# Block-sparse attention with a gated feed-forward: batches 1 to 3 go from masked full scores to gathered key blocks

## The chip, the cores and the metric

The kernel runs on one core of a Trainium2 chip. The core has a matrix engine (PE), three elementwise engines (DVE, ACT and POOL) and a queue engine (SP); SP, ACT and POOL also issue DMA transfers. Each engine works through its own instructions in program order and waits on semaphores for the others. The metric is the device time of one execution in microseconds (us); lower is better. A measurement of this kernel can tell a difference of about 0.2% from none.

## The reference

There are 4 batches, 8 heads, 768 positions and a head size of 64. Positions form 24 blocks of 32. A query block sees its own block and its two neighbours, the first and the last block, and three sampled blocks; the queries of the first and last block see everything. The attention output, as 3072 rows of 512, goes through an RMS norm and a gated feed-forward of width 1536.

```python
    scores = scale * np.matmul(q, k.transpose(0, 1, 3, 2))
    mask = np.abs(blk_i - blk_j) <= window            # window = 1
    mask = mask | (blk_i == 0) | (blk_j == 0) | (blk_i == n_blocks - 1) | (blk_j == n_blocks - 1)
    for qb in range(n_blocks):
        for kb in sampled_blocks[qb]:
            mask[qb * block:(qb + 1) * block, kb * block:(kb + 1) * block] = True
    scores = np.where(mask, scores, -1000000000.0)
    attn = np.exp(scores - np.max(scores, axis=-1, keepdims=True))
    attn = attn / (np.sum(attn, axis=-1, keepdims=True) + 1e-09)
    out = np.matmul(attn, v)
    ...
    rms = np.sqrt(np.mean(x * x, axis=-1, keepdims=True) + 1e-06)
    xn = x / rms * rms_g
    g = xn @ w_gate
    silu = g * (1.0 / (1.0 + np.exp(-g)))
    return silu * (xn @ w_val) @ w_out
```

## The kernel before, in words

All scores are computed, and the mask is part of the matmul: below the 64 rows of a head, `KT` and `QT` hold 24 more rows, which say of each key its block and give each query -65536 for every block that it does not see. A matmul over 88 rows so yields masked scores, and the exponential makes the masked ones zero.

Tokens are handled in groups: batch 0 in three groups of 2 tiles of 128 tokens, batches 1 to 3 in two groups of 3 tiles each (`groups`). For a group and a head, `scores` multiplies six blocks of 128 keys (L330, 256 or 384 columns) and takes the exponential on ACT (L333, 768 columns a piece). One head later `pv` multiplies the exponentials with `Vp`, whose column 64 is one, so that column 64 of `op` is the sum (L341, 66 columns); DVE divides (L350, L351). Sums of squares (L375, DVE), the power -1/2 (L383, POOL) and a scaling (L395, L403) give `xs`, which is transposed into `xg` by DMA from SP, or on PE for the first groups and the last.

The feed-forward of a group is cut into pieces by `ffn_pieces`: `gate` (four matmuls, L442, then tanh on ACT, L446), `val` (four matmuls, L453, then two DVE operations into `hps`, L457 and L459) and `down` (three matmuls into `yp`, L470, and at last ACT's copy and the store). Gate, value and down results share three PSUM buffers (`ps_f`). The order is written out by hand: the pieces of the group that was finished last are spread over the "positions" between the scores and values of the present one (`enter`, `position`), so that PE always has work while ACT takes exponentials.

q and k of batch 0 are transposed on PE. Those of batches 1 to 3 are loaded by POOL, transposed by DMA from SP (`turn`, L300) and moved into `KT` and `QT` by two more DMAs each (`place`, L308). v is loaded by POOL and cast by DVE (`cast_v`, L120). `KT`, `QT` and `Vp` have two buffers each, by the parity of the batch.

Of the kernel before, what the change touches and what calls it, by code (L numbers as in the profile page):

```python
# [18 lines left out]
def kernel(  # L19
# [11 lines left out]
):  # L31

    nc = tc.nc
    P = 128
    B, H, S, D = q.shape
    NB = S // 32  # L40
    NC = S // P
    DM = H * D
    DFF = moe_w_gate.shape[1]
    KD = DM // P
    MASKV = -65536.0
    SCALE = 1.0 / (D ** 0.5)
    NRND = sampled_blocks.shape[1]
    NF = DFF // P
    HC = NC // 2
    TGM = HC * P  # L50

    groups = [(0, c, 2) for c in range(0, NC, 2)]
    groups += [(b, c, HC) for b in range(1, B) for c in range(0, NC, HC)]
    FIRST = NC // 2
    KR = D + NB
    NP = H // 2
    VW = D + 2
    VS = D + 16
# [6 lines left out]
    work = ctx.enter_context(tc.tile_pool(name="work", bufs=1))  # L65
    ps_f = ctx.enter_context(tc.tile_pool(name="ps_f", bufs=3, space=bass.MemoryType.PSUM))
# [3 lines left out]


    qbf, kbf, vraw, qrest = {}, {}, {}, {}

    def load_q0(pr, lo, hi):

        if lo == 0:
            t = qbf[(0, pr)] = ld.tile([P, 2, 2 * D], BF16, name="q0", tag="q0", bufs=3)
        else:
            t = ld.tile([P, 2, NC * D], BF16, name="qbf", tag="qbf", bufs=4)[:, :, lo * D:]
            qrest[(0, pr)] = t  # L80
        nc.gpsimd.dma_start(  # L81
            out=t, in_=q[0, 2 * pr:2 * pr + 2].rearrange(
                "e (p c) d -> p e (c d)", p=P)[:, :, lo * D:hi * D])

    def load_one(b, pr, store, t=None):
        src, name = (k, "kbf") if store is kbf else (q, "qbf")
        if t is None:
            t = ld.tile([P, 2, NC * D], BF16, name=name, tag=name, bufs=4)
        nc.gpsimd.dma_start(  # L89
            out=t,  # L90
            in_=src[b, 2 * pr:2 * pr + 2].rearrange("e (p c) d -> p e (c d)", p=P))
        store[(b, pr)] = t

    def load_qk(b, pr):
        load_one(b, pr, kbf)
        load_one(b, pr, qbf)

    def load_v(b, pr):
        t = ld.tile([P, 2, NC, D], FP32, name="vraw", tag="vraw" if b else "vraw0",
                    bufs=2 if b else 4)  # L100
        nc.gpsimd.dma_start(  # L101
            out=t, in_=v[b, 2 * pr:2 * pr + 2].rearrange("e (p c) d -> p e c d", p=P))
        vraw[(b, pr)] = t
# [3 lines left out]
    wo = persist.tile([P, NF, DM], BF16, name="wo")  # L107
    def load_gv(lo, hi):

# [5 lines left out]
    KT = [persist.tile([P, H, S], BF16, name=f"KT{i}") for i in range(2)]  # L115
    QT = [persist.tile([P, H, S], BF16, name=f"QT{i}") for i in range(2)]
    Vp = [persist.tile([P, H, NC, VS], BF16, name=f"Vp{i}") for i in range(2)]

    def cast_v(b, pr, eng):
        eng.tensor_copy(  # L120
            out=Vp[b % 2][:, 2 * pr:2 * pr + 2, :, 0:D], in_=vraw.pop((b, pr)))
# [3 lines left out]
    samp_i = const.tile([32, NB * NRND * 2], I32, name="samp_i")  # L125
# [3 lines left out]
    nc.scalar.dma_start(out=samp_i[0:NB, :], in_=s32.to_broadcast([NB, NB * NRND * 2]))  # L129
    first = {}  # L130
    for h in range(2):
        for which, src in ((0, k), (1, q)):
            f32 = ld.tile([P, NC * D], FP32, name="first", tag="turned", bufs=4)
            cols = 2 * D if which else NC * D
            nc.sync.dma_start(
                out=f32[:, 0:cols],
                in_=src[0, h].rearrange("(p c) d -> p (c d)", p=P)[:, 0:cols])
# [5 lines left out]
    def halves(which, b):  # L143

        if which == 0:
            return KT[b % 2][0:D].rearrange("p h (w c s) -> p h w c s", w=2, s=P)
        return QT[b % 2][0:D].rearrange("p h (c w s) -> p h w c s", w=2, s=P)

    def first_turn(src, which):
        dt = src.dtype  # L150
        t = ps_f.tile([P, HC, P], dt, name="tfirst", tag="ff")
        for cc in range(1 if which else HC):
            nc.tensor.transpose(
                out=t[:, cc, :], in_=src[:, 2 * cc * D:(2 * cc + 2) * D],
                identity=ident32 if dt == FP32 else ident)
        return t

    def first_copy(h, which, t, w, copy):
        hi = 1 if which else HC
        copy(out=halves(which, 0)[:, h, w, 0:hi, :], in_=t[w * D:(w + 1) * D, 0:hi])  # L160

    idle = const.tile([P, 512], BF16, name="idle")
# [3 lines left out]

# [15 lines left out]
    ki_i = work.tile([32, S], I32, name="ki_i", tag="hps", bufs=2)  # L182
# [16 lines left out]
    for i in range(2):  # L199
        nc.vector.memset(Vp[i][:, :, :, D:VW], 1.0)  # L200
# [12 lines left out]
    kind = KT[0][D:KR, 0, :]  # L213
    qmask = QT[0][D:KR, 0, :]
# [3 lines left out]

# [9 lines left out]
    for lo, hi in ((2, 4), (4, H)):  # L228
        nc.sync.dma_start(out=KT[0][D:KR, lo:hi, :],
# [20 lines left out]
    def spread_queries(third, lo):  # L250
# [3 lines left out]
            out=QT[0][D:KR, lo:H, c_lo:c_hi],  # L254
# [5 lines left out]
    def copy_rows(T, m, lo, hi, c_lo, c_hi):  # L260

        nc.vector.tensor_copy(
            out=T[0][D:KR, lo:hi, c_lo:c_hi],
# [10 lines left out]
    copy_rows(QT, qmask, 1, 2, 0, 2 * P)  # L274
    copy_rows(KT, kind, 1, 2, 0, S)
    nc.sync.dma_start(out=rmsr, in_=moe_rms_g.rearrange("(h p) -> h p", p=P))

    def transpose_qk(b, pr, which, lo, hi, spare, copy):

        src = (qrest if lo else qbf if which else kbf)[(b, pr)]
# [7 lines left out]
        view = halves(which, b)[:, 2 * pr:2 * pr + 2]  # L290
# [3 lines left out]
    turned = {}  # L294

    def turn(b, pr, which):

        src = (kbf if which == 0 else qbf).pop((b, pr))
        t = ld.tile([P, 2, HC, P], BF16, name="turned", tag="turned", bufs=4)
        nc.sync.dma_start_transpose(  # L300
            out=t.rearrange("p e c s -> p (e c) s"), in_=src.rearrange("p e x -> p (e x)"))
        turned[(b, pr, which)] = t

    def place(b, pr, which):
        t = turned.pop((b, pr, which))
        view = halves(which, b)[:, 2 * pr:2 * pr + 2]
        for w in range(2):
            nc.sync.dma_start(out=view[:, :, w], in_=t[w * D:(w + 1) * D])  # L308

    def place_half(b, pr, which, w):  # L310
        t = turned[(b, pr, which)]
        view = halves(which, b)[:, 2 * pr:2 * pr + 2]
        nc.vector.tensor_copy(out=view[:, :, w], in_=t[w * D:(w + 1) * D])
        if w:
            del turned[(b, pr, which)]

    def ex_tile(n):
        t = work.tile([P, NC * TGM], BF16, name="ex", tag="ex", bufs=3)
        return t[:, 0:NC * n * P].rearrange("p (j t) -> p j t", j=NC)

    def scores(grp, h, part, ex):

        b, c0, n = grp
        tg = n * P
        nj = 2 if n == HC else 3
        st = ps_s.tile([P, 1024], FP32, name="st", tag="st")
        at = st.rearrange("p (j t) -> p j t", t=512 if n == HC else tg)
        for e in range(nj):
            jt = nj * part + e
            nc.tensor.matmul(  # L330
                out=at[:, e, 0:tg], lhsT=KT[b % 2][0:KR, h, jt * P:(jt + 1) * P],
                rhs=QT[b % 2][0:KR, h, c0 * P:c0 * P + tg], start=True, stop=True)
        nc.scalar.activation(  # L333
            out=ex[:, nj * part:nj * (part + 1), :], in_=at[:, 0:nj, 0:tg], func=AF.Exp,
            scale=SCALE)

    def values(grp, h, ex, op):
        b, c0, n = grp
        for it in range(n):
            for jt in range(NC):  # L340
                nc.tensor.matmul(  # L341
                    out=op[:, it, 0:VW], lhsT=ex[:, jt, it * P:(it + 1) * P],
                    rhs=Vp[b % 2][:, h, 2 * (jt % HC) + jt // HC, 0:VW], start=(jt == 0), stop=(jt == NC - 1))

    def pv(grp, h, ex, stage):
        n = grp[2]
# [149 lines left out]
    fill = []  # L496
# [334 lines left out]
```

## Time and profile before

| | |
|---|---|
| median of 3 runs | 309.09 us (308.88 to 309.12) |
| the profiled execution | 309.93 us |
| its span, first to last instruction | 308.2 us |
| mean granted PE clock | 0.998 |
| matmuls | 2843 |
| DMA moved | 36.71 MB, mean 119 GB/s |

The profile is of one execution, and its span is a little shorter than the time, which also holds what lies around the first and last instruction. A line of a group of instructions gives the line of the code, engine, operation, output and inputs with shapes and count, then the busy time in us and the mean length of one in ns, then the idle time of the engine ahead of them and what ended it. A matmul's own length contains the way through the array; how far apart matmuls start is read from the chain or the timeline. A line of a stage gives busy times of all engines in a stretch.

### The profile page before, as it was taken

What the parts mean: (1) busy time and instruction counts of PE and PEld (TensorE: products, weight loads), DVE (VectorE), ACT (ScalarE), POOL (GpSimd) and SP (SyncE); (2) the same over time, 40 slices, a digit from 0 to 9 for tenths busy, and PEclk for the clock granted to TensorE, in tenths of its full rate; (3) what the DMA queues carried; (4) which work ended last, traced back from release to release, by engine and by line L of the source; (5) the groups of instructions that cost most, each with busy time, mean ns of one, the idle gap of its engine ahead of it and who ended that gap; (6) DMA issues with size and microseconds to landing.
All of it is one profiled execution on the core that took longest, in us unless ns stands there. A gap on an engine that the chain in (4) does not pass through costs nothing.

```text
span 308.2 us, 7249 instructions
## 1 busy us (share of the span) xinstructions
PE 299.9 (97%) x2843; PEld 198.9 (65%) x2863; DVE 203.6 (66%) x561; ACT 204.8 (66%) x330; POOL 54.7 (18%) x81
## 2 busy tenths in 40 slices
PE   8889999999999999999999999999999999999995
PEld 6676886985787566656666566655666566655653
DVE  7788884885578567763768457682767546675860
ACT  4886775776888677757776676676767667732331
POOL 9846201042220212012200122010000100010000
PEclk9999999999999999999999999999999999999999
DMA  7999999999999478526673379614000130002002
GB/s 124 276 210 201 208 215 151 171 173 245 218 205 146 112 154 162 109 48 189 113 156 85 81 176 148 140 25 139 16 2 0 42 115 2 0 5 100 2 0 103
DMA packets 61082, 36.71 MB, mean 119 GB/s; under 512 B 38348, under 2 KB 56640, under 8 KB 61048
## 3 DMA queue, kind: packets, MB, share of 16 engines
q0 software_dynamic: 17120, 17.90, 32.7%
q1 hardware_dynamic: 43892, 18.35, 27.5%
q8 instruction: 22, 0.36, 0.5%
q14 instruction: 12, 0.10, 0.1%
q10 hardware_dynamic: 36, 0.01, 0.0%
HBM read 28.59 MB, written 6.29 MB: 113 GB/s over the span
## 4 chain that ended last, share of the span: by engine, by line
PE 91%; POOL 3%; DMA 3%; DVE 2%; issue 1%; ACT 0%; POOLq 0%
PE gp L442 21%; PE vp L453 20%; PE yp L470 20%; PE st L330 18%; PE op L341 11%; DMA qbf<-in_q_dram 3%; POOL kbf L89 1%; PE tx L424 1%; POOL vraw L101 1%; POOL q L81 1%; DVE junk L375 1%; DVE stage L368 0%; PE tqk L287 0%; DVE xs L403 0%; POOL ki_i L183 0%
## 5 line engine op out<-in xcount | busy, mean ns | idle before, releaser
L333 ACT ACTIVATE ex<-st 128x768 bf16<-128x768 f32 x186 | 150.0, 813 | 53.7 <-PE st L330 51.9
L330 PE MATMUL st<-QT,KT 88*128 88x384 bf16 (+1 forms) x432 | 93.9, 309 | 1.4 <-DVE QT L292 1.0
L442 PE MATMUL gp<-xg,wg 128*128 128x384 bf16 (+1 forms) x432 | 80.8, 307 | 0.0
L453 PE MATMUL vp<-xg,wv 128*128 128x384 bf16 (+1 forms) x432 | 80.2, 307 | 0.0
L457 DVE SCALAR_TENSOR_TENSOR u<-th,gp 128x384 bf16<-128x384 bf16 (+1 forms) x108 | 54.8, 508 | 38.1 <-ACT th L446 36.6
L470 PE MATMUL yp<-wo,hps 128*128 128x512 bf16 (+1 forms) x283 | 71.9, 369 | 0.9
L446 ACT ACTIVATE th<-gp 128x384 bf16<-128x384 f32 (+1 forms) x108 | 49.1, 454 | 27.8 <-PE gp L442 27.5
L459 DVE TENSOR_TENSOR hps<-u,vp 128x384 bf16<-128x384 bf16 (+1 forms) x108 | 55.1, 510 | 11.3
L330 PEld LDWEIGHTS <-KT 88*128 88x128 bf16 x432 | 41.5, 98 | 26.1 <-DVE QT L292 2.0
L453 PEld LDWEIGHTS <-wv 128*128 128x128 bf16 x432 | 40.6, 97 | 20.6 <-issue 0.2
L442 PEld LDWEIGHTS <-wg 128*128 128x128 bf16 x432 | 40.1, 97 | 20.5 <-issue 0.3
L341 PEld LDWEIGHTS <-ex 128*128 128x128 bf16 x1116 | 42.8, 97 | 8.4 <-issue 0.2
L341 PE MATMUL op<-Vp,ex 128*128 128x66 bf16 x1116 | 44.9, 193 | 0.0
L470 PEld LDWEIGHTS <-hps 128*128 128x128 bf16 x300 | 27.6, 97 | 22.6 <-DMA wo<-in_moe_w_out_dram 0.3
L383 POOL TENSOR_TENSOR rstd<-ssq,mhalf 128x3 f32<-128x3 f32 (+1 forms) x9 | 7.4, 817 | 143.1 <-DVE ssq L375 143.1
L350 DVE RECIPROCAL rz<-op 128x3 f32<-128x3 f32 (+1 forms) x64 | 11.2, 174 | 24.0 <-PE op L341 23.7
L476 ACT ACTIVATE yo<-yp 128x512 f32<-128x512 f32 (+1 forms) x25 | 14.4, 577 | 15.4 <-PE yp L470 15.4
L351 DVE TENSOR_TENSOR stage<-op,rz 128x192 bf16<-128x192 f32 (+1 forms) x64 | 21.8, 341 | 2.2
L101 POOL DMA_DIRECT2D vraw<-in_v_dram x16 | 11.8, 739 | 59.3 <-DVE Vp L120 55.7
L375 DVE CUSTOM_DVE_ANT_0 junk<-stage 128x448 bf16<-128x448 bf16 (+1 forms) x24 | 14.7, 611 | 0.5
L395 DVE SCALAR_TENSOR_TENSOR xs<-stage,rstd,gain 128x512 bf16<-128x512 bf16 x15 | 10.4, 746 | 4.4 <-POOL rstd L383 4.4
L89 POOL DMA_DIRECT2D qbf<-in_q_dram x12 | 8.6, 721 | 16.8 <-DMA turned<-qbf 15.4
(71 smaller groups left out, 112.2 us busy)
## 6 DMA issues: line engine op xcount, KB each, us to landing
vraw<-in_v_dram POOLq DMA_DIRECT2D x16, 384.0 KB, 5.2
out_dram<-yo SPq DMA_DIRECT2D x23, 256.0 KB, 2.3
kbf<-in_k_dram POOLq DMA_DIRECT2D x15, 192.0 KB, 6.0
qbf<-in_q_dram POOLq DMA_DIRECT2D x12, 192.0 KB, 6.3
KT<-turned SPq DMA_DIRECT2D x24, 96.0 KB, 3.7
QT<-turned SPq DMA_DIRECT2D x22, 96.0 KB, 2.9
wg<-in_moe_w_gate_dram POOLq DMA_DIRECT2D x4, 384.0 KB, 10.7
wv<-in_moe_w_val_dram POOLq DMA_DIRECT2D x4, 384.0 KB, 12.1
```

Source lines behind the costliest of these rows:

```text
L101: nc.gpsimd.dma_start(out=t, in_=v[b, 2 * pr:2 * pr + 2].rearrange("e (p c) d -> p e c d", p=P))
L330: nc.tensor.matmul(out=at[:, e, 0:tg], lhsT=KT[b % 2][0:KR, h, jt * P:(jt + 1) * P], rhs=QT[b % 2][0:KR, h, c0 * P:c0 * P + tg], start=Tru ...
L333: nc.scalar.activation(out=ex[:, nj * part:nj * (part + 1), :], in_=at[:, 0:nj, 0:tg], func=AF.Exp, scale=SCALE)
L341: nc.tensor.matmul(out=op[:, it, 0:VW], lhsT=ex[:, jt, it * P:(it + 1) * P], rhs=Vp[b % 2][:, h, 2 * (jt % HC) + jt // HC, 0:VW], start=(j ...
L351: nc.vector.tensor_tensor(out=stage[:, 0:n, h * D:(h + 1) * D], in0=op[:, 0:n, 0:D], in1=rz[:, 0:n].unsqueeze(2).to_broadcast([P, n, D]), ...
L375: nc.vector.tensor_tensor_reduce(out=junk[:, 0:hi - lo], in0=part, in1=part, scale=1.0, scalar=(e["ssq"][:, it:it + 1] if lo else DM * 1e- ...
L442: nc.tensor.matmul(out=gp[:, 0:tg], lhsT=wg[:, c, f * P:(f + 1) * P], rhs=xg[:, c, 0:tg], start=(c == 0), stop=(c == KD - 1))
L446: nc.scalar.activation(out=th[:, 0:tg], in_=gp[:, 0:tg], func=AF.Tanh, scale=0.5)
L453: nc.tensor.matmul(out=vp[:, 0:tg], lhsT=wv[:, c, f * P:(f + 1) * P], rhs=xg[:, c, 0:tg], start=(c == 0), stop=(c == KD - 1))
L457: nc.vector.scalar_tensor_tensor(out=u[:, 0:tg], in0=th[:, 0:tg], scalar=1.0, in1=gp[:, 0:tg], op0=ALU.add, op1=ALU.mult)
L459: nc.vector.tensor_tensor(out=hps[:, f, 0:tg], in0=u[:, 0:tg], in1=vp[:, 0:tg], op=ALU.mult)
L470: nc.tensor.matmul(out=yp, lhsT=hps[:, f, tt * P:(tt + 1) * P], rhs=wo[:, f, lo:hi], start=(f == 0), stop=(f == NF - 1))
```

## The change

Batch 0 stays as it was. Batches 1 to 3 are cut into chunks of four query blocks: five regular chunks of four neighbouring blocks (2 to 5, 6 to 9, ...) and one edge chunk with blocks 0, 23, 1 and 22, which makes 18 chunks (`chunks`).

Keys are laid out in pairs: `KT` now has an even position's 64 values in partitions 0 to 63 and the next one's in 64 to 127, so a block of 32 keys is 16 columns. For each query block, 8 blocks of keys are copied side by side into 128 columns of `kg`: three sampled, the first, three of the window, the last. The window and the first and last block are copied by DVE (`gather_k`); the sampled blocks by ACT or POOL with an address from a register (`sampled_k`), which `addresses` loads earlier. `gather_q` (DVE) lays the queries out twice in `Qd`, once for each half of the partitions, with zeros in the other, so one matmul of 128 x 128 by 64 columns scores a query block against its 256 keys (`scores`, four bursts a chunk with an exponential of 512 columns each). An edge chunk scores its two full rows against all keys.

Values are cast into `Vs`, stored to a table in DRAM (`table`), and POOL gathers 128 rows of 2112 bytes for each query block by indirect DMA with the indices `vidx` (`gather_v`). A sampled block that is seen already, or sampled twice, points to rows of zeros, sums included. `values` multiplies with 32 columns of weights at a time: `op[j * 32:(j + 1) * 32]` for the four blocks in turn, 66 columns each.

A chunk is scored in one iteration, its values are taken in the next, which has ten positions, and feed-forward groups are of 2, 3, 3, 3, 3, 2 and 2 chunks. q and k of batches 1 to 3 are transposed on PE and copied by DVE (batch 1) or ACT. Loads of v for batches 2 and 3 move from POOL to SP. `KT0`, `QT0` and `Vp` of batch 0 share memory with buffers of the sparse part.

```diff
-    KT = [persist.tile([P, H, S], BF16, name=f"KT{i}") for i in range(2)]
-    QT = [persist.tile([P, H, S], BF16, name=f"QT{i}") for i in range(2)]
-    Vp = [persist.tile([P, H, NC, VS], BF16, name=f"Vp{i}") for i in range(2)]
+    KT = [paired(wide_k[:, 0:half]), persist.tile([P, H, NT], BF16, name="KT1")]
+    QN = [paired(wide_k[:, half:2 * half]), persist.tile([P, H, NT], BF16, name="QN1")]
+    Vs = [persist.tile([P, NC, H, VW], BF16, name=f"Vs{i}") for i in range(2)]
+    vgs = [persist.tile([P, QB, 2 * HV], BF16, name=f"vg{i}") for i in range(3)]
...
+    def gather_v(i, js=range(QB)):
+        b, qbs = chunks[i]
+        for j in js:
+            if qbs[j] not in (0, NB - 1):
+                nc.gpsimd.indirect_dma_start(
+                    vgs[i % 3][:, j, :], None, vtab[b][:],
+                    bass.IndirectOffsetOnAxis(ap=vidx[:, qbs[j]:qbs[j] + 1], axis=0))
...
+    def scores(i, part):
+        b, qbs = chunks[i]
+        wide = qbs[0] == 0
+        heads = H // bursts(i)
+        st = places["s"].tile([P, 512], FP32, name="st", tag="st")
+        at = 0
+        for h in range(part * heads, (part + 1) * heads):
+            of = [(KT[b % 2][:, h, cc::HC], j) for cc in range(HC) for j in range(2)] if wide else []
+            of += [(kgs[i % 2][:, h, j, :], j) for j in range(2 if wide else 0, QB)]
+            for lhsT, j in of:
+                nc.tensor.matmul(
+                    out=st[:, at:at + UN], lhsT=lhsT,
+                    rhs=Qd[i % 2][:, h, :, :, j * HB:(j + 1) * HB].rearrange("p a w s -> p (a w) s"),
+                    start=True, stop=True)
+                at += UN
...
+        def mm(h, j, lhsT, rhs, n, of):
+            at = (h % 4) * VW
+            nc.tensor.matmul(out=op[j * BLK:(j + 1) * BLK, h // 4, at:at + VW], lhsT=lhsT, rhs=rhs,
+                             start=(n == 0), stop=(n == of - 1))
...
+            if not wide:
+                for w in range(2):
+                    for j in range(QB):
+                        mm(h, j, ex[:, j, w, :], vg[:, j, w, h, :], w, 2)
+                continue
...
+        else:
+            do(0, lambda: values(i - 1))
+            do(0, lambda: squares(i - 1, i > 4))
+            do(2, lambda: rms_power(i - 1))
+            do(4, lambda: x_turned(i - 1))
+        if i < NCH:
+            n = bursts(i)
+            for part in range(n):
+                do(1 + part * 4 // n, lambda part=part: scores(i, part))
+        if b + 1 < B and 1 <= s <= NP:
+            pr = s - 1
+            do(0, lambda: cast_v(b + 1, pr, dve))
+            do(3, lambda: turn(b + 1, pr, 0, act))
+            do(7, lambda: turn(b + 1, pr, 1, act))
...
+            if s == NP:
+                do(1, lambda: zero_rows(b + 1))
+                do(1, lambda: table(b + 1))
+        if nx is not None:
+            at = 6 if nx == 1 else 0
+            do(at, lambda: gather_k(nx, dve))
+            do(at + 1, lambda: gather_q(nx, dve))
+            kact, kpool = sampled_k(nx, "act"), sampled_k(nx, "pool")
...
+            do(1, lambda: gather_v(nx, range(0, 1)))
+            do(3, lambda: gather_v(nx, range(1, QB)))
...
+        if b + 1 < B and s < NP:
+            do(7, lambda: load_v(b + 1, s))
+            do(7, lambda: load_kq(b + 1, s))
```

## The prediction

> **What bounds the kernel now.** I read the busy times first, then a stage in the steady part, then the chain that ended last, then the groups of instructions with their shapes apart.
>
> ```profile
> PE 299.9 (97%) x2843; PEld 198.9 (65%) x2863; DVE 203.6 (66%) x561; ACT 204.8 (66%) x330; POOL 54.7 (18%) x81
> 133.90:169.50 35.60, 35.49 (x324) 21.84 (x324) 22.55 (x58) 24.82 (x39) 5.21 (x7) 1.00 0.56 122
> 292.00:308.20 16.20, 13.00 (x80) 7.62 (x78) 5.51 (x10) 3.93 (x8) 0.00 (x0) 0.96 0.13 49
> ```
>
> The second and third lines are stages: length, then busy time of PE, weight loads, DVE, ACT and POOL, the granted clock, DMA share and GB/s. One group of 384 tokens takes 35.6 us and PE has no hole in it, at full clock. DVE (63%) and ACT (70%) have slack, POOL idles. The kernel is bound by the number and width of its matmuls, except for the first 9 us and the last 3.
>
> ```profile
> 18.31 0.75 PE op L341 x24
> 165.43 0.65 PE vp L453 x4
> 169.56 1.30 PE yp L470 x6
> 74.01 0.39 PE L424 MATMUL tx<-ident,xs 128*128 128x128 bf16 x4
> 74.23 0.81 PE L470 MATMUL yp<-wo,hps 128*128 128x512 bf16 x3
> ```
>
> The first three are pieces of the chain (start, length, what). They give PE's pace: 384 columns 0.65/4 = 162.7 ns, 512 columns 216 ns, the 66-column value matmul 31 ns; four 128-column transposes take 74.23 - 74.01 = 0.22 us, 55 ns each. Check on the stage: 48 score and 96 gate/value matmuls at 162.7 are 23.4, 36 `yp` at 216 are 7.8, and the 4.4 left over 144 `op` is 30.9 ns each. A 256-column matmul is then about 109 ns.
>
> ```profile
> L333 ACT ACTIVATE ex<-st 128x768 bf16<-128x768 f32 x186 | 150.0, 813 | 53.7 <-PE st L330 51.9
> L446 ACT ACTIVATE th<-gp 128x384 bf16<-128x384 f32 x72 | 35.3, 490 | 21.3 <-PE gp L442 21.2
> L160 ACT CAST QT<-tfirst 64x128 bf16<-64x128 f32 x2 | 0.5, 255 | 0.0
> L313 DVE COPY QT<-turned 64x768 bf16<-64x768 bf16 x2 | 0.7, 350 | 0.0
> L457 DVE SCALAR_TENSOR_TENSOR u<-th,gp 128x384 bf16<-128x384 bf16 x72 | 39.8, 552 | 32.5 <-ACT th L446 31.4
> masks.py:199 POOL TENSOR_SCALAR_AFFINE_SELECT ident<-ident 128x128 f32<-128x128 f32 x1 | 0.3, 296 | 0.1
> L383 POOL TENSOR_TENSOR rstd<-ssq,mhalf 128x2 f32<-128x2 f32 x3 | 2.2, 720 | 17.3 <-DVE ssq L375 17.3
> L89 POOL DMA_DIRECT2D qbf<-in_q_dram x12 | 8.6, 721 | 16.8 <-DMA turned<-qbf 15.4
> kbf<-in_k_dram POOLq DMA_DIRECT2D x15, 192.0 KB, 6.0
> vraw<-in_v_dram POOLq DMA_DIRECT2D x16, 384.0 KB, 5.2
> ```
>
> These are the prices for the new work (busy us, mean ns), and, in the last two lines, the time from issue to landing of a load.
>
> **The change, part by part, on PE.** Batch 0 keeps its work up to 66 us, where its last scores end.
>
> 1. *Scores of batches 1 to 3.* Gone: 288 matmuls of 384 columns, 288 x 162.7 = 46.9 us. New: 672 of 64 columns (32 in each of 15 chunks, 64 in each of 3 edge chunks). Nearest row is the 66-column one: 30.9 x 64/66 = 30 ns, 20.2 us. Net -26.7. Ends: 17.9 us by bare column rate (0.416 ns a column, from 216/162.7) and 20.8.
> 2. *Values.* Gone: 864 at 30.9, 26.7 us. New: 1344 (64 a chunk, 128 an edge chunk), also 66 columns wide, but each writes 32 partitions, and four neighbours write the four quarters of `op`. The trace has no such matmul. If they run one after another each costs what the row shows, 30.9 ns, 41.5 us; if the four quarters run beside each other a set of four costs one, 7.7 ns each, 10.3 us. Beyond the upper end lies the weight load's own 97 ns, if it were no longer hidden. I take the geometric middle, 15.4 ns, 20.7 us: they share no output, but each still brings its own weight load. Net -6.0, ends -16.4 and +14.8.
> 3. *Change of shape* on PE around the 18 value bursts: between nothing and one latency of that matmul (193 ns in its group) on either side, 0 to 6.9; taken 3.5.
> 4. *Transposes of q and k.* Before, the SP queue did them by DMA (24 transposes, 46 placements). Now PE does 144 at 55 ns: +7.9. Eight fewer for `xs`: -0.4.
> 5. *Feed-forward.* Same columns, in groups of 2 and 3 tiles: +0.2, nothing.
>
> Sum on PE: -26.7 - 6.0 + 3.5 + 7.9 - 0.4 = **-21.7 us**. A PE with no hole would give a span of 308.2 - 21.7 = 286.5.
>
> The Trainium skill prices the values otherwise: TensorEngine Tiling (Array Packing), Performance Considerations, says that a matmul costs about 60 cycles however narrow it is, by estimate 25 ns and 33.6 us for 1344, which would make the span 299 without a hole. The same page's Key Properties let tiles on different parts of the array run in parallel, which is the 10.3 us end. No row here shows either.
>
> **The other engines, per chunk.** PE after the change has about 198 us for 18 iterations, near 10.9 us each, so whatever needs less is hidden.
> - ACT: 144 exponentials of 768 become 84 of 512 (between the 490 and 813 rows, 0.60 us): -67; 108 copies of one sampled block (0.255 row) +27.5; 19 copies out of the transposes (as 768 wide, 0.81) +15.4; 14 squares +8.4; tanh +2. Net -13.6, to about 191. Some 8.5 us a chunk.
> - DVE: window and edge copies (1536 and 512 elements; the 350 ns row of 768 gives 0.55 and 0.28) +14; 84 query copies (0.22 to 0.29) +23; larger `stage`, fewer squares and casts -26; five turn copies, indices, memsets +10; feed-forward +2. Net about +23, to 226. Some 8.3 us a chunk.
> - POOL: 66 gathers. Their issue is not in the trace: at least the plain issue, 0.72; at most perhaps twice the dearest repeated one (1.02 for `wo`), 2.0. I take 1.0, since a plain issue hardly grows with its rows. 90 sampled-block copies: 0.2 to 0.87, taken as the 0.296 row. Two small operations a chunk, 1.3. Eight `v` loads go to SP. A regular chunk: 4 + 1.2 + 1.3 + 0.6 = 7.1 us.
> - SP loses some 57 us of transposes and placements and gains some 25 short issues; it is no bound. DMA: gathers bring 17.8 MB more; the removed transposes and placements moved about 9 (24 of 192 KB, 46 of 96 KB).
>
> So PE stays the bound, but with four engines at 65 to 80% and in order, not without holes. The new waits:
> - *Start of the sparse part.* The first scores need POOL's casts, the table's store and landing, four gathers, a window copy and 12 sampled copies, in one queue. 0 to 8 us, taken 3.
> - *k for the next batch* is issued on POOL at position 7 and PE turns it at position 3 of the next iteration: six positions, 6.5 us, for a landing of 6.0, behind three gathers in the same queue. PE itself waits. Eight times 0 to 2 us; taken 3 in all.
> - *v for the next batch*: SP at position 7, DVE cast at position 0. Three positions, the value burst and `stage` are some 5.2 us, the landing 5.2. What is late holds the window copy, the query copies, `u` and `hps` on DVE, and then the three buffers of gate and value results on PE. Taken with the next.
> - *Bursts on DVE*: reciprocal, `stage`, cast, window copy and four query copies are 3 us in a row, where the three buffers give PE about 1.7 us of lead. 0 to 1 us an iteration; taken 3.
> - *Edge chunks*: eight exponentials where PE has about four positions of other work, 2 buffers; 0 to 8 in all, taken 2.
>
> Together 11 us of new holes: span 297.5. The profiled execution took 309.93 for a span of 308.2, and the median of the runs is 309.09, 0.9 above that span. Forecast: **298 us**.
>
> **Rivals.**
> - *A: the quarters do not overlap (slower).* Values at 30.9 ns add 20.8 to the forecast: 319. It decides from about 23.7 ns a matmul (1344 x 8.3 ns = 11 us, the forecast's gain). For it: the nearest row, and one weight load each. Against: four disjoint outputs. The skill's 60 cycles, as above, would be 298 + 12.9 = 311 and fall here. Chance 0.17.
> - *B: POOL becomes the bound (slower).* A chunk needs 3.1 + 4x us for x a gather; above x = 1.9 that passes 10.7 and PE waits for `op` inputs. At x = 2.2 it is 11.9 x 18, some 20 us more: 318. Against: the flat issue rows. The skill's GPSIMD Engine Reference, Key points, has POOL share its SBUF interfaces with fast DVE operations; no run here shows it. The copies are 1.7 us a chunk on DVE, so even then POOL needs 8.8. Chance 0.07.
> - *C: late loads and bursts (slower).* The upper ends of the waits for k, v and DVE add up to 30 instead of 6: 310 to 322. For it: four full gathers ahead of k. Chance 0.10.
> - *D: the holes close and the quarters overlap.* 286.5 - 10.4 + 4 and the offset: 281. Chance 0.10.
>
> **How the numbers follow.** Forecast 0.56 (its own range 286 to 308), D 0.10, A 0.17, B 0.07, C 0.10. Faster: 0.56 + 0.10 = 0.66. Slower: 0.31, with 0.03 out of the three slower cases for within 0.2%, which is about what a measurement of this kernel can tell from no change. Range: 281, at D, to 321, the upper part of A to C; about 0.1 lies on either side.
>
> **What would show it.** Right: the value matmuls start under 20 ns apart; PE busy per iteration near 10.5 us; POOL under 80% in the sparse part; ACT below 200 us. Wrong: `op` at 31 ns or worse; PE waiting on the transposes for a `kbf` landing; DVE waiting on `vraw`; gathers over 1.9 us on POOL; holes of more than 11 us in the sparse part, or a first sparse score that waits for POOL beyond 8 us.

## The result and the profile after

| | before | after |
|---|---|---|
| median | 308.99 us (308.63 to 309.12, 4 runs) | 348.03 us (345.7 to 349.05, 4 runs) |
| profiled execution, its span | 309.93, 308.2 us | 347.89, 346.1 us |
| PE busy, PE idle in the span | 299.9, 8.3 us | 290.0, 56.1 us |
| mean granted PE clock | 0.998 | 0.969 |

The ratio is 1.1255, with an interval of 1.1198 to 1.1312: 39 us slower, where 298 us were forecast. Some executions of a kernel run some per cent longer at a lower clock, and the medians below leave them out (that of POOL, v and bank is then the 320.16 us of a single run, where later expectations start from 323.5).

From the page of the changed kernel: the busy times, the chain that ended last by engine, three groups of instructions, and the load of v.

```profile
PE 290.0 (84%) x3959; PEld 198.6 (57%) x3959; DVE 224.0 (65%) x597; ACT 188.7 (55%) x437; POOL 158.6 (46%) x273
...
PE 45%; DVE 23%; DMA 15%; issue 7%; ACT 5%; POOL 3%; POOLq 1%; SPq 1%; DVEq 0%; ACTq 0%
...
L725 PE MATMUL vp<-xg,wv 128*128 128x256 bf16 (+1 forms) x480 | 84.1, 298 | 27.4 <-DVE u L729 25.6
...
L495 POOL DMA_INDIRECT vg<-vtab,vidx x66 | 67.3, 1020 | 30.1 <-ACT ex L513 14.7
...
vraw<-in_v_dram SPq DMA_DIRECT2D x8, 384.0 KB, 4.6
```

No engine is over 84% now, and the chain has only 45% of PE, where it had 91%. What replaced PE in the chain is DVE and DMA. POOL, with its gathers at 1.02 us, is not the bound.

The waits of PE (us in all, how many, the longest):

```profile
PE vp L725 <- DVE u L729: 25.6, 23, 3.7
PE tqk L442 <- DVE stage L529: 12.1, 4, 9.4
PE st L601 <- ACT ex L609: 3.4, 6, 1.2
```

Before, no line of this list was over 1.2 us in all. Two stretches show what stands behind the two large lines. The first is the tail of batch 0. First the stretch, with columns as in the prediction; then the chain that ended last, inside it (start, length, what).

```profile
50.00:66.00 16.00, 6.57 (x45) 4.01 (x43) 3.68 (x8) 2.92 (x4) 6.32 (x7) 0.68 0.37 73
```

```profile
48.68 0.62 POOLq L416
...
49.37 0.95 POOLq L416
...
50.38 0.94 POOLq L416
...
51.38 1.19 POOLq L416
...
53.87 0.59 POOL gain L858
...
54.50 1.80 POOL Qd L866
56.31 0.77 POOL Vs L425
57.08 0.71 POOL rstd L559
...
57.81 1.74 DVE xs L567 x2
59.55 0.08 DVE rz L528
...
59.65 0.30 DVE stage L529
...
60.09 1.01 PE tqk L442 x8
```

POOL takes its jobs in order. The power for the normalisation of a batch 0 group (L559) stands behind six loads of registers with the addresses of the sampled blocks (`addresses`, L416, between 48.7 and 53.3 us), the load of `gain`, the clearing of `Qd` and a cast. DVE waits 9.0 us for that power, its `stage` stands behind it, and PE, whose turn needs the bank that `stage` frees, waits 9.4.

The second stretch is in the sparse part. Again the chain:

```profile
194.83 1.27 SPq L678
...
196.20 6.99 DMA vraw<-in_v_dram
203.19 1.56 issue
204.75 0.56 DVE Vs L425
205.31 0.48 DVE kg L458
...
206.81 0.29 DVE Qd L485
...
207.13 0.56 DVE u L729
...
207.74 0.81 PE vp L725 x4
208.55 0.28 PE st L601 x8
208.83 1.28 PE gp L714 x4
...
213.40 0.65 PE gp L714 x4
```

v is asked for behind SP's transpose of `xs` and lands 7 us later; DVE's cast starts 1.6 us after that. Behind the cast stand the window copy, four query copies and only then `u`; PE has used its three banks and waits 3.1 us. And then the four matmuls of `gp` take 1.28 us instead of 0.65: the granted clock has fallen. The last but two figure of a stretch is that clock. The first four stretches below begin behind the holes of 9.4, 3.6, 3.7 and 3.1 us, the fifth behind one of 2.98 us:

```profile
60.00:66.00 6.00, 5.91 (x41) 3.91 (x42) 1.58 (x4) 2.32 (x3) 0.23 (x1) 0.56 0.00 0
105.00:109.00 4.00, 3.58 (x36) 2.79 (x36) 3.25 (x10) 1.88 (x4) 3.39 (x4) 0.65 0.79 219
144.40:148.40 4.00, 3.98 (x34) 3.16 (x34) 2.86 (x7) 1.85 (x6) 2.57 (x9) 0.65 0.71 266
207.70:211.70 4.00, 3.96 (x22) 2.13 (x22) 3.06 (x6) 1.66 (x5) 1.06 (x3) 0.61 1.00 183
180.00:184.00 4.00, 3.64 (x40) 2.39 (x39) 3.72 (x10) 2.52 (x6) 3.46 (x7) 1.00 0.74 199
```

The length of a hole alone does not decide it. In the kernel with POOL free and v early (experiment 5) the clock also falls behind holes of 2.48 and 1.98 us:

```profile
53.90:57.90 4.00, 4.00 (x26) 2.70 (x27) 1.57 (x3) 1.51 (x2) 0.12 (x1) 0.57 0.17 57
133.00:137.00 4.00, 3.85 (x31) 2.98 (x31) 2.88 (x7) 1.54 (x5) 3.10 (x10) 0.59 0.62 181
```

The Trainium skill, in TensorE: Matmul & The Clock Gate, "HAM oscillation", says that PE's clock is throttled to half once PE waits longer than about 3.4 us. The traces agree on the half, with twice the time per matmul behind such a hole; they differ on the length, as 2 us were enough in one kernel and 2.98 us were not in another.

In sum: PE's busy time fell by 9.9 us, though some 7 us of it is slower clock (an estimate: in every half microsecond, PE's busy time times what its clock lacks to full; before, nothing). At full clock its work fell by about 17 us, where 21.7 were forecast. PE's idle time grew by 47.8 us. With the clock, the new holes cost some 55 us where 11 were forecast.

### The profile page after: what moved, and what is told of

It is laid out like the page before. It is cut to its first block, busy times and chain, and to the rows that moved or that the text cites. A ratio compares the mean times of both kernels' runs of the same rounds, so it can differ in the third digit from the quotient of the medians.

```text
span 346.1 us, 10011 instructions
## 1 busy us (share of the span) xinstructions
PE 290.0 (84%) x3959; PEld 198.6 (57%) x3959; DVE 224.0 (65%) x597; ACT 188.7 (55%) x437; POOL 158.6 (46%) x273
## 4 chain that ended last, share of the span: by engine, by line
PE 45%; DVE 23%; DMA 15%; issue 7%; ACT 5%; POOL 3%; POOLq 1%; SPq 1%; DVEq 0%; ACTq 0%
PE yp L743 13%; PE vp L725 10%; DMA vraw<-in_v_dram 9%; PE gp L714 9%; DVE u L729 5%; DMA qbf<-in_q_dram 5%; PE op L624 3%; DVE hps L733 3%; PE st L510 3%; PE st L601 2%; DVE stage L647 2%; ACT ex L609 2%; PE tqk L442 2%; ACT th L718 1%; DVE xs L676 1%
## 5 line engine op out<-in xcount | busy, mean ns | idle before, releaser
L725 PE MATMUL vp<-xg,wv 128*128 128x256 bf16 (+1 forms) x480 | 84.1, 298 | 27.4 <-DVE u L729 25.6
L714 PE MATMUL gp<-xg,wg 128*128 128x256 bf16 (+1 forms) x480 | 85.0, 300 | 0.3 <-DMA xg<-xs 0.2
L495 POOL DMA_INDIRECT vg<-vtab,vidx x66 | 67.3, 1020 | 30.1 <-ACT ex L513 14.7
L718 ACT ACTIVATE th<-gp 128x256 bf16<-128x256 f32 (+1 forms) x120 | 51.4, 429 | 43.6 <-PE gp L714 38.3
L729 DVE SCALAR_TENSOR_TENSOR u<-th,gp 128x256 bf16<-128x256 bf16 (+1 forms) x120 | 56.5, 471 | 25.1 <-ACT th L718 21.9
L733 DVE TENSOR_TENSOR hps<-u,vp 128x256 bf16<-128x256 bf16 (+1 forms) x120 | 56.9, 474 | 15.1 <-PE st L601 2.1
L609 ACT ACTIVATE ex<-st 128x512 bf16<-128x512 f32 x84 | 49.3, 598 | 26.7 <-PE st L601 18.0
L513 ACT ACTIVATE ex<-st 128x768 bf16<-128x768 f32 x42 | 33.3, 812 | 13.7 <-PE st L510 13.5
L748 ACT ACTIVATE yo<-yp 128x512 f32<-128x512 f32 (+1 forms) x25 | 14.4, 576 | 21.7 <-PE yp L743 21.6
L510 PE MATMUL st<-wide_q,wide_k 88*128 88x256 bf16 x144 | 24.3, 282 | 1.6 <-DVE wide_q L336 1.2
L624 PEld LDWEIGHTS <-ex 128*32 128x32 bf16 x1344 | 13.7, 95 | 7.3 <-issue 7.0
L510 PEld LDWEIGHTS <-wide_k 88*128 88x128 bf16 x144 | 13.5, 101 | 6.2 <-DVE wide_q L336 2.6
L624 PE MATMUL op<-vg,ex 128*32 128x66 bf16 x1056 | 15.6, 196 | 1.0 <-issue 1.0
```

The source lines that it names most:

```text
L495: nc.gpsimd.indirect_dma_start(vgs[i % 3][:, j, :], None, vtab[b][:], bass.IndirectOffsetOnAxis(ap=vidx[:, qbs[j]:qbs[j] + 1], axis=0))
L510: nc.tensor.matmul(out=at[:, e], lhsT=KT0[0:KR, h, jt * P:(jt + 1) * P], rhs=QT0[0:KR, h, c0 * P:(c0 + 2) * P], start=True, stop=True)
L513: nc.scalar.activation(out=ex[:, 3 * part:3 * (part + 1), :], in_=at[:, 0:3], func=AF.Exp, scale=SCALE)
L609: nc.scalar.activation(out=ex.rearrange("p (u s w) -> p u s w", s=HB, w=2), in_=st.rearrange("p (u w s) -> p u s w", s=HB, w=2), func=AF.E ...
L624: nc.tensor.matmul(out=op[j * BLK:(j + 1) * BLK, h // 4, at:at + VW], lhsT=lhsT, rhs=rhs, start=(n == 0), stop=(n == of - 1))
L714: nc.tensor.matmul(out=gp[:, 0:tg], lhsT=wg[:, c, f * P:(f + 1) * P], rhs=xg[:, c, 0:tg], start=(c == 0), stop=(c == KD - 1))
```

## The experiments

Three theories were held against each other. **Theory 1, late arrivals**: a few single things come late (POOL's loads ahead of the power; v, k), and with them away the forecast is met. **Theory 2, bursts**: DVE's 3 us of chunk work in a row is what holds `u`. **Theory 3, no slack**: in the feed-forward, gate, tanh, `u` and `hps` go round three PSUM banks; where less attention work lies between the pieces, this round itself is as long as PE's work for a piece, and whatever DVE or ACT does besides stalls PE.

The kernels ran in five sets, each on one chip; the second and third set had the same chip. The kernel before took 308.99 to 310.55 us everywhere, but variants of the changed kernel differ from set to set (experiment 9), so only neighbours in a set, or on the same chip, are compared. The changed kernel itself was not run in any set; in set 1 the kernel with pairs in a quarter (348.39 us, only the order of its value matmuls is changed) stands for it.

| set (kernel before) | kernels, median in us |
|---|---|
| 1 (310.55) | POOL free 341.49, v early 339.82, coarse spread 353.77, pairs in a quarter 348.39 |
| 2 (309.12) | quarters in a row 353.14, fourth bank 346.03, POOL and v 324.52, POOL, v and bank 320.16 |
| 3 (309.04), same chip as 2 | with k early 321.92, with DVE spread 328.91, with freed tail 321.10, all three 322.76 |
| 4 (309.18) | five edits 332.63, without gate product 319.62, the kernel before without it 309.47, squares on ACT 333.30 |
| 5 (309.33) | four edits again 336.04, five edits again 331.63 |

**1. POOL's queue.** Six of POOL's register loads go from the group before to the last head of the last batch 0 group, and `Qd` is cleared by DVE.

```diff
+            if h == 7:                       # gi == 2
+                for i in range(1, PB):
+                    addresses(i, NRND - 1)
...
-                for i in range(1, PB):       # gi == 1, h == 5
-                    addresses(i, NRND - 1)
...
+                nc.vector.memset(Qd[0], 0.0)  # gi == 1, h == 6
-                nc.gpsimd.memset(Qd[0], 0.0)  # gi == 2, h == 0
```

> Moves nothing but POOL's six address loads for chunks 1 to 5 (from batch 0's second group to the end of its third) and the zeroing of Qd (to DVE, one group earlier). Theory 1, late data in an in-order queue: the 9.4 us hole of PE from 50.7 to 60.1 us is POOL reaching the power of the second group's norm 9 us late, so the hole shrinks to 2 to 4 us, the half clock behind it goes too, and the time falls by 8 to 12 us from 348.0, to 336 to 340. Rival, the hole is the landing of the q and k loads, which only happens to end at the same time: it stays, and the time is 345 to 349.

Measured: 341.49 us (340.35 to 342.62), 6.9 less than its neighbour with the reordered values, a little under the 8 to 12 expected. The same stretch, and two lines of waits of this kernel:

```profile
50.00:66.00 16.00, 12.53 (x117) 8.16 (x114) 8.18 (x21) 5.64 (x11) 4.22 (x6) 0.89 0.48 128
```

```profile
PE tqk L442 <- DVE stage L529: 5.2, 4, 2.6
...
DVE Vs L425 <- DMA vraw<-in_v_dram: 13.0, 6, 3.5
```

The hole shrinks from 9.4 to 2.6 us (PE busy 12.5 us of 16, not 6.6), but part of that came back later: DVE's wait for v, 10.8 us in the changed kernel (7.0, and the 3.8 behind the load of the chain above), rose to 13.0.

**2. v earlier,** at position 1 of an iteration and not 7.

```diff
-            do(7, lambda: load_v(b + 1, s))
+            do(1, lambda: load_v(b + 1, s))
```

> One position number: v of the next batch is loaded at position 1 instead of 7, nine positions ahead of its cast instead of three. Theory 1: DVE no longer waits for the landing in the eight iterations with a cast (seen: 0.3 to 2.2 us of idle each, and 3 to 3.7 us of idle on PE behind the longest), so the idle time of DVE ahead of the cast goes from 11 us to under 2, PE's four holes of 3 us and more go, with the half clock behind them, and the time falls by 10 to 18 us, to 330 to 338. Rival, DVE has too much in a row and the wait only hides that: PE waits for u as long as before (25.6 us in 23 waits), and the time falls by less than 5 us.

Measured: 339.82 us (338.9 to 340.74), 8.6 less than that neighbour, under the 10 to 18 expected. DVE no longer waits for `vraw`. But PE still waits for `u`:

```profile
PE vp L725 <- DVE u L729: 16.9, 23, 2.5
```

As often as before (23 times), though 8.7 us less in all. So the load is one cause and not the only one.

**3. Bursts, coarsely.**

```diff
-            do(at, lambda: gather_k(nx, dve))
-            do(at + 1, lambda: gather_q(nx, dve))
+            do(6, lambda: gather_k(nx, dve))
+            do(7, lambda: gather_q(nx, dve))
```

> The window copy and the query copies for the next chunk go to positions 6 and 7 in every iteration, instead of 0 and 1, so they no longer stand between the stage, the cast and the first u of an iteration. Theory 2, bursts on DVE: PE's waits for u fall by half or more and the time falls by 8 to 15 us, to 333 to 340. Theory 1 alone: the cast's wait stays in front of u, so PE's holes of 3 us and more stay and the time falls by 0 to 4 us; it may rise, if copies that come late hold up the scores of the next chunk.

Measured: 353.77 us, 5.4 *more* than the neighbour; PE waited 29.1 us for `u`, 27 times. Taking the copies out of the burst and putting them between feed-forward pieces made it worse. Theory 2 in this form falls. My reading, which no run tests by itself, is that the burst lies partly beside PE's values and scores, and away from them it costs more.

**4. Do the quarters overlap?** First the two key halves of a block stand behind each other, then (second kernel) all 16 matmuls of a quarter.

```diff
-                for w in range(2):
-                    for j in range(QB):
-                        mm(h, j, ...)
+        for j in range(QB):                  # the second kernel: outermost
+            for h in range(H):
+                for w in range(2):
+                    mm(h, j, ...)
```

> The value matmuls of a query block follow each other in pairs into the same quarter of op, instead of going round the four quarters; work and operands are the same. If the 9.7 ns a matmul (64 in 0.62 us) come from the four quarters running beside each other, pairs run two deep at most and a burst of 64 takes 1.2 to 2.0 us (19 to 31 ns each), 15 regular chunks cost 9 to 20 us more on PE, of which some falls into holes: 352 to 366. If a matmul with 32 columns of weights is simply short, the burst stays at 0.62 us and the time at 348.

> All matmuls of one quarter stand behind each other: the block loop is outermost, then heads, then the two halves of the keys, in the regular chunks; nothing else changes. Theory 'a value matmul is short by itself' (it streams 66 columns): a burst of 64 keeps its 0.62 to 0.69 us, time 346 to 350. Rival 'the four quarters must be interleaved': with neighbours always in the same quarter a matmul costs what the score matmul of 128 rows costs, 29 ns, the burst of 64 grows to about 1.9 us, 18 bursts cost about 22 us, time 360 to 372.

Measured: 348.39 us with pairs, 353.14 with whole quarters in a row. The first two lines are from the chain of the changed kernel, the next two from that of the second kernel, with whole quarters in a row.

```profile
127.14 0.62 PE op L624 x64
239.26 1.57 PE op L624 x128
```

```profile
114.72 1.74 PE op L624 x64
150.62 1.74 PE op L624 x64
```

64 value matmuls take 0.62 us (9.7 ns each) when neighbours write different quarters, and 1.74 us (27.2 ns) when all neighbours write the same one. So the quarters do run beside each other, about 2.8 at a time, and pairs are close enough for that. PE had 16 us more to do in the second kernel's bursts (15 x 1.1 us). Its span is only 4.1 us longer than that of the changed kernel (350.2 against 346.1, not the same set), and PE's idle time 8.5 us shorter (47.6 against 56.1): part of the longer bursts fell into holes. The time of 360 to 372 us expected for this case was a miss.

**5. A fourth bank, and both gains together.** Every second gate result goes to the bank of the turns, and the turns of the sparse part take one of the three others:

```diff
+            if more and f % 2:
+                gp = ps_o.tile([P, 512], FP32, name="gp", tag="ot")
+            else:
                 gp = gate_pool.tile([P, 512], FP32, name="gp", tag="ff")
```

> In the feed-forward groups of the sparse chunks every second gate result goes to the bank that the turns of keys and queries use (they take one of the three others instead), so that four banks and not three carry gate and value results; nothing else changes. Theory 3 (with less attention work between the pieces, the round of gate, tanh, product and free bank has no slack left, so each late ACT or DVE job stalls PE): vp waiting on u falls from 25.6 us to under 15, time 333 to 341. Rival (only the late loads of v make these waits): vp on u stays at 22 us or more, time 345 to 350.

> Both single changes that gained (POOL's address loads moved ahead of the batch 0 tail, v loaded six positions earlier), nothing else. If they are separate holes: 348.0 less 6.5 less 8.2 = 333, 331 to 336. If they compete (in the first kernel the wait on v rose as the hole of POOL went): under 331. If one hides the other: 338 to 341.

> The two changes and the fourth bank together. Theory 3: 8 to 13 us less than the two changes alone, 320 to 326, vp waiting on u under 8 us. Rival: the fourth bank gives under 3 us on top.

Measured: 346.03, 324.52 and 320.16 us (the last in one run). PE's waits in the kernel with the fourth bank alone:

```profile
PE vp L728 <- DVE u L732: 12.1, 8, 3.5
PE tqk L442 <- DVE stage L529: 9.9, 3, 9.0
PE tqk L442 <- DVE hps L736: 5.4, 3, 4.7
```

The waits for `u` halve, as theory 3 says, but the time is only about 2 us under the 348.03 of the changed kernel, in the range of the rival. Turns that share the banks now wait for `hps`, and more goes to the clock: PE idles 6.5 us less (49.6 against 56.1), while 14.3 us of its busy time go to the lower clock and not 7.2 (estimated as above). In the last batch, where nothing is turned and the granted clock is 1.00 in both, the bank can be seen alone. From one value burst to the next, the six intervals from chunk 11 to 17 took 12.0, 10.6, 9.4, 13.6, 16.0 and 12.3 us with three banks and 11.3, 10.0, 9.4, 13.1, 14.8 and 12.0 with four (the second and first kernel, same chip): 3.3 us less. On top of POOL and v the bank gave 4.4 us, neither the 8 to 13 of theory 3 nor the rival's under 3.

POOL and v together give 21.5 us against the kernel with the bank alone (346.03), but 9.3 of these are that kernel's slower clock (14.3 against 5.0 us). Against the changed kernel the span falls by 22.5 us (346.1 to 323.6), and PE's idle time from 56.1 to 38.2 us, where each edit alone left 51.2 and 49.7. That is more than the two apart, as if each hole had hidden part of the other, and the wait for v in experiment 1 is a sign of it; but the single edits ran on another chip than the two together, so it is not shown.

**6. k and q earlier, DVE spread finely, the tail freed.** On the kernel with POOL, v and bank. The tail: the casts of v one head later, behind the power, and all turns of that group in `ps_f`.

```diff
-            do(7, lambda: load_kq(b + 1, s))
+            do(0, lambda: load_kq(b + 1, s))
```

```diff
-            do(0, lambda: squares(i - 1, i > 4))
+            do(1, lambda: squares(i - 1, i > 4))
...
-            do(0, lambda: cast_v(b + 1, pr, dve))
+            do(2, lambda: cast_v(b + 1, pr, dve))
...
-            do(at, lambda: gather_k(nx, dve))
-            do(at + 1, lambda: gather_q(nx, dve))
+            do(at or 3, lambda: gather_k(nx, dve))
+            do(at + 1 if at else 5, lambda: gather_q(nx, dve, (0,)))
+            do(at + 1 if at else 6, lambda: gather_q(nx, dve, (1,)))
```

> On top of the kernel with both changes and the fourth bank (323.5 us, 320.2 in its faster run): k and q of the next batch asked for at position 0 and not 7 of the iteration before they are turned. Theory 1 (loads that land behind the work that needs them): PE's 4.3 us of waits on kbf go, with the half clock behind them: 315 to 320. Rival (POOL's queue is what holds them, and the earlier issue holds up the gathers instead): 321 to 327.

> On top of the same kernel: DVE's work for a chunk, at positions 0 and 1 so far, is spread one piece to a position (normalising 0, squares 1, cast of v 2, keys 3, queries 5 and 6). Theory 3 in its form 'any job between two products stalls PE': vp waiting on u falls from 9.4 us to 4 to 6, time 316 to 321. Rival (as in the coarser spread before, which cost 6 us): the jobs only stall other pieces, 322 to 328.

> On top of the same kernel, in the last group of batch 0 only: POOL's four casts of v start one head later, behind the power that the normalisation waits for, and the turns of keys and queries never take the bank of the attention results. Theory (that one bank and POOL's order hold PE between 50 and 86 us, where it is idle for 5.6 us and 3.6 us go to the lower clock): 315 to 319. Rival (the turns take a bank from gate and value results instead): 322 to 326.

> The three edits together. If the holes are separate and each was rightly named: 303 to 311, at or under the kernel before. Rival (what is left is the round of gate, tanh, product and bank, whatever comes late): 315 or more.

Measured: 321.92, 328.91, 321.10 and 322.76 us, none under the 320.16 of the base's one run. k and q earlier gained nothing that can be seen. The freed tail did what it should in its place (PE's busy time stands behind the comma):

```profile
50.00:66.00 16.00, 15.78 (x190) 12.48 (x189) 11.76 (x29) 10.19 (x18) 4.46 (x6) 1.00 0.52 144
...
86.00:99.00 13.00, 9.49 (x120) 7.45 (x106) 8.86 (x24) 5.93 (x16) 11.78 (x23) 0.74 0.88 210
```

Full from 50 to 66 us; but the first sparse iteration then waits (clock 0.74, DMA engines at 0.88), among others 1.7 us for `u` and 1.75 us for a `kbf`, and the whole is no faster than its base. Spreading DVE's work, the second time and finely, cost 7 us against the kernel with k early, and in it PE waits for `u` ahead of gates too (7.2 us, where that kernel has 3.1). With all three the kernel is no faster than with one, so the 303 to 311 us of separate holes is a miss. It agrees with theory 3: no place tried in an iteration let a DVE job go free.

**7. Take half the round away.** On the kernel with five edits (POOL, v, bank, k and q, tail), and on the kernel before, DVE does one product per feed-forward piece instead of two.

```diff
-            u = work.tile([P, TG], BF16, name="u", tag="u", bufs=3)
-            nc.vector.scalar_tensor_tensor(
-                out=u[:, 0:tg], in0=th[:, 0:tg], scalar=1.0, in1=gp[:, 0:tg], op0=ALU.add, op1=ALU.mult)
...
-            nc.vector.tensor_tensor(out=hps[f][:, 0:tg], in0=u[:, 0:tg], in1=vp[:, 0:tg], op=ALU.mult)
+            nc.vector.scalar_tensor_tensor(
+                out=hps[f][:, 0:tg], in0=th[:, 0:tg], scalar=1.0, in1=vp[:, 0:tg], op0=ALU.add, op1=ALU.mult)
```

> Five edits together and no spreading of DVE's work: POOL's address loads ahead of the tail of batch 0, v asked for at position 1, the fourth bank, k and q asked for at position 0, casts and turns of the tail of batch 0 out of the way. Separate holes: 316 to 319 (323.5 less 1.6 less 2.4). Rival (one queue behind all): 320 to 323.

> The kernel with the five edits, and the product with the gate left out of the computation in all feed-forward groups: one DVE product of (tanh plus 1) and value instead of two products, so that a gate's bank is free after the tanh; DVE has some 57 us less to do. Theory 3 (the round has no slack in the sparse part): 12 to 18 us less than the five edits alone, 300 to 306. Rival (the rest is loads and gathers): under 5 us less.

> The same product left out of the kernel before. Theory 3: there the round has slack beside the attention matmuls (PE waited 0 us on a product), so the gain is under 3 us, at the end alone: 306 to 309. Rival (the round costs PE time in any mix): 295 to 302.

Measured, on one chip: five edits 332.63 us, without the product 319.62, so 13.0 less, inside the 12 to 18 of theory 3. The five edits themselves missed their 316 to 319 on this chip (experiment 9). The kernel before: 309.18 and 309.47, ratio 1.0021 with an interval of 0.9997 to 1.0046, so no gain. One stage of the kernel before, with the product and without it:

```profile
99.00:150.00 51.00, 50.84 (x470) 31.27 (x473) 31.90 (x83) 35.63 (x56) 8.29 (x11) 1.00 0.58 126
...
99.00:150.00 51.00, 50.84 (x470) 31.29 (x469) 23.31 (x63) 34.97 (x56) 7.43 (x10) 1.00 0.59 125
```

The same of the changed kernel with five edits, with the product and without it:

```profile
99.00:150.00 51.00, 37.77 (x648) 28.31 (x649) 33.78 (x91) 29.86 (x78) 31.75 (x55) 1.00 0.62 167
...
99.00:150.00 51.00, 43.18 (x780) 30.89 (x782) 25.71 (x71) 28.44 (x73) 31.65 (x56) 0.93 0.71 178
```

In both kernels DVE loses 51 us of work (203.6 to 152.4, 224.8 to 173.4). In the one PE was full and stays full; in the other PE's waits for DVE's products, `u` and `hps`, fall from 21.3 to 7.0 us, and the time by 13. This is the clearest result of the study: the same DVE work was free before and costs time after. It takes a step out of the round and work off DVE at once, so it does not tell a long round from a crowded DVE; only the fourth bank of experiment 5 changes the round alone, and it gave less.

**8. Squares on ACT.**

```diff
-            do(0, lambda: squares(i - 1, i > 4))
+            do(0, lambda: squares(i - 1, True))
```

> The five edits, and the squares of the first five sparse chunks on ACT and not on DVE (5 x 0.77 us off DVE, 5 x 0.63 us onto ACT). Theory 3: 2 to 4 us less, 312 to 316, as each of these stands ahead of a product that PE waits for. Rival: no change of over 1 us, or the tanh is late instead.

Measured: 333.30 us against 332.63: no gain. A miss for theory 3 in its simple form: five jobs of 0.77 us off DVE are not worth 0.77 each. ACT, which must bring the tanh and the exponentials, got them. In the trace PE's waits for `u` fall by 3.9 us (18.6 to 14.7), those of the scores for `ex` rise by 1.5 (5.2 to 6.7), and the lower clock takes more (mean 0.985 against 0.990).

**9. The chip.**

> The kernel with POOL's loads, early v, the fourth bank and early k and q, unchanged, beside the one with five edits. If the program sets the time: 320 to 324 as before. If the place sets it: 330 to 335, as the five edits had there, or both near 320.

> The kernel with five edits, unchanged. If the program sets the time (the freed tail of batch 0 brings the sparse part into a worse phase): 331 to 334, 9 to 12 us more than its neighbour in this call. If the place sets it: within 4 us of its neighbour.

Measured: 336.04 and 331.63 us, 4.4 apart, just beyond the 4 expected of the place. The same program with four edits had taken 321.92 on the chip of sets 2 and 3, so 14 us lie between the two sets, while the kernel before stayed at 309.0 and 309.3. Each chip was used at one time only (sets 2 and 3 within some minutes), so the chip and the hour are not told apart. From value burst to value burst the sixteen intervals up to chunk 16 differ by 10 us in all, most in three of the first nine (13.5 and 15.2, 10.8 and 13.5, 12.2 and 13.7 us) and in one of the last batch, where nothing is loaded (14.8 and 16.9 us). On the slower chip PE stops five times between 140 and 225 us for 0.44 to 0.76 us without a wait that the profile shows, in and near the bursts of small matmuls; on the other no such stop is over 0.16 us. That is 2.7 us; another 3 us are lower clock (6.3 us of PE's busy time against 3.3, estimated as above). What the rest is, and why, was not settled.

No variant with the whole computation beat the kernel before. The best that ran more than once, the freed tail with 321.10 us, is 3.9% slower (ratio 1.039, 1.037 to 1.041).

## Why the prediction was wrong

The step that failed is **"together 11 us of new holes"**: it was some 55 us, 47.8 of idle PE and 7 of lower clock. The sum on PE came out near (17 us of the 21.7), but not term by term: at the measured prices below it would be 28 us, and what lies between was not measured. PE's busy time also holds the way through the array behind the last matmul ahead of each stop, and the changed kernel has more stops.

- *Scores, 30 ns*: eight start in 0.23 us, 29 ns each. Right.
- *Values, 15.4 ns between 7.7 and 30.9*: 9.7 to 10.5 ns in regular chunks, 12.3 in edge chunks; 15 x 0.65 and 3 x 1.57 us are 14.5 us, not 20.7. The end "four beside each other" was nearer than the middle. Rival A is out. Of the two sentences that the prediction takes from the Trainium skill, TensorEngine Tiling (Array Packing), the one on tiles in parallel (Key Properties) agrees with the 9.7 ns of neighbours in different quarters, and the 60 cycles a matmul (Performance Considerations; 25 ns by the prediction's estimate) do not. The 27.2 ns of neighbours in the same quarter don't test the 60 cycles, as 66 columns at the 0.416 ns of the prediction are 27.5 ns.
- *Transposes, 55 ns*: six in 0.34 us, 57 ns. Right. *Shape change*, 3.5 us: no run measured it by itself.
- *ACT 191, DVE 226 us, gather 1.0 us*: 188.7, 224.0, 1.02. Right, and rival B with POOL as the bound is out (46% busy).
- *Start of the sparse part, 3 us*: the wait came one stage earlier and was 9.4 us. The queue named was the right one, POOL's, but the list of what stands in it left out the register loads of `addresses`, and the step "batch 0 keeps its work up to 66 us" did not ask who of batch 0 waits behind POOL. Experiment 1 shows it.
- *k, 3 us in all*: not among PE's large waits in the changed kernel; 0.3 us there and up to 5.2 in a kernel with other holes closed (DVE spread finely). Small, as forecast.
- *v and DVE bursts, 3 us in all*: mis-sized most. DVE waited 10.8 us for v and PE 25.6 us for `u`. The chain of "what is late" was named word for word (window copy, query copies, `u`, banks), but priced by averages: landing 5.2 us against 5.2 us of cover. In the trace the load stood behind SP's 1.27 us for a transpose and landed in 7.0.
- *Edge chunks, 2 us*: 3.4 us of waits on `ex`. About right.
- *Not in the sum at all*: that the clock falls behind holes (some 7 us), and that the round of gate, tanh, `u`, `hps` and bank, or DVE's work in it, has no slack once the attention work between pieces is gone. The prediction did compare "1.7 us of lead" with 3 us of DVE work, but took 0 to 1 us an iteration and 3 us in all. Experiment 7 puts about 13 us on one of the two products, in the variant with five edits; how much it is in the changed kernel itself was not measured.

Rival C had the mechanism of the loads, at a chance of 0.10 and up to 322 us. Its upper ends were still too low: it had no term for POOL ahead of batch 0's power, none for the clock and none for the round.

What stays open: of the 50 us above the forecast, POOL and v explain about 22, and the product about 13 as measured in a later variant on another chip, so these two need not add up. What the rest is, some 15 us, was not shown; part of it differs from set to set.

## What to carry to other kernels

When a change takes work from the engine that is the bound, ask first what that work was covering: a chain through two or three engines and a few PSUM banks, which cost nothing beside other matmuls, can become the pace once they are gone. Busy shares of 55 to 65% do not show this; compare the length of one round with the bound engine's remaining work for a round, for each stage. Then list every queued instruction, register loads too, ahead of the one that the bound engine waits for, and count a hole of 2 us or more twice, once for itself and once for a clock that may be at half for some microseconds behind it.

## What the runs showed of the hardware

- Narrow matmuls (66 columns) into 32 partitions: 9.7 ns each with neighbours in different quarters, 27.2 ns in the same one.
- Loading the registers that address the sampled blocks kept POOL for 0.3 to 1.2 us a load (in the changed kernel's trace, between 48.7 and 53.3 us).
- PE's granted clock fell to half behind holes of PE from 1.98 to 9.4 us, and did not behind one of 2.98 us.
- The same program differed by 14 us (4%) between two chips (at two times) on which a PE-bound one agreed within 0.1%.
